# Local attention with a spectral gate on one core: sine tables moved ahead of batch 0, other PSUM banks for its transposes, pairs 2 and 3 loaded by another queue

## Chip, cores and metric

The kernel runs on one core of one Trainium2 chip, in one launch. The metric is the device time in microseconds (us), taken as the median of several runs; the profile is one further execution with the hardware profiler on.

## The reference

Two operators are joined. The first is attention over q, k, v of shape (4 batches, 8 heads, 768 positions, 64 dims). A position sees the 8 global keys and the last 96 keys (its own among them), and a distance times a slope of the head is taken off the scores:

```
scores = q @ k^T / sqrt(64) - slope[h] * dist        (only kept keys)
a = softmax(scores);  x = (a @ v), heads side by side  -> (4, 768, 512)
```

The second is a gate with a circular convolution along the 768 positions, done with a Fourier transform of each of the 512 columns:

```
x1, x2, x3 = split(x @ w_proj)                        # w_proj 512 x 1536
conv = irfft(rfft(x2) * rfft(filter_fft))
out = (x1 * conv * x3) @ w_out
```

All inputs and the output are float32 in HBM. On the chip the work is done in float16 with float32 sums.

## The kernel before

**Stages.** The work goes by batch. For a batch, `attention` (line 378) makes the 512 x 768 tile `xT`, and `hyena` (line 544) makes the output from it. The emitter writes attention of batch 0 alone, then four times hyena of batch b together with attention of batch b+1. `weave` (line 304) takes such streams, cut into steps by their `yield`s, and writes their steps in turn, each stream in even paces over its share of the stage. With hyena of batch 0 a third stream runs, `filter_stage` (line 328): it makes the sine tables `fwd` of the Fourier transform, the spectrum of the filter and the inverse tables. No planner stands behind this: each engine carries out its instructions in just the order that the program writes them, and waits at the first that is not ready.

**Attention.** Four pairs of heads follow each other. For a pair, PE transposes q and k (`transpose_q`, `transpose_k`) into PSUM, ACT copies out `QT` and DVE copies out `KT`. `weights` makes the scores of seven key blocks in three groups `sc(i, 0..2)`, ACT takes the exponential into `E` (line 499), and DVE multiplies it with the mask one step later (lines 508 and 511). `values` multiplies with v (lines 519 and 524), DVE divides by the row sum (lines 528 and 529), `transpose_x` turns the result, and ACT copies it to `xT`. All transposes use one PSUM bank, tag "tr" with one buffer; three banks with the tag "mm" serve projections and the Fourier transform, one double bank "s" the scores, two "av" the values.

**Batch 0.** It starts cold. `load_first` issues eight loads of 384 KB from SP (q and k of four pairs, float32), and `cast_first` has DVE bring each to float16 (line 143). Six staging buffers hold them. The masks are made on the way from a table of distances that POOL and DVE build (`distances`, `masks`). v of batch 0 comes from POOL's DMA queue, which casts to float16 as it goes: eight DMAs (lines 105 and 108). When they have all landed, DVE copies the global rows into six further places (line 425), and only then can `values` start. Behind v, POOL issues the three loads of `w_proj` (line 163), then k and q of batch 1, the filter `fl`, v of batch 1, and so on. On POOL's queue a DMA waits for the landing of the eighth one before it. Matmuls on a tile of zeros (`busy`, line 270) fill PE's gaps in batch 0.

**Sine tables.** In four parts a = 0..3, PE makes the products frequency times position as integers in PSUM (`dft_angles`, lines 241 to 248), ACT rounds them over S with a large constant (line 252), DVE takes the remainder in two instructions (lines 257 and 260, put some steps later by `after`), and ACT takes the sine (line 268). Exp and Sin need different tables in ACT, so each change of the function is an ACT_TABLE_LOAD.

Of the kernel before, what the change touches and what calls it, by code (L numbers as in the profile page):

```python
# [17 lines left out]
P = 128  # L18
NG = 8
# [25 lines left out]
class Fused:  # L45
# [79 lines left out]
    def load_first(self):  # L125


        nc, D = self.nc, self.D
        self.first = []
        for hp in range(4):  # L130
            hs = slice(2 * hp, 2 * hp + 2)
            for eng, src in ((nc.sync, self.q), (nc.sync, self.k)):
                st = self.stage([P, 2, 6, D])
# [13 lines left out]

    def stage(self, shape):
        t = self.mp.tile([P, 768], F32, tag="stg", bufs=6)
# [25 lines left out]
    def distances(self):  # L175
# [3 lines left out]
        dg = self.mp.tile([P, n], F32, tag="p1", name="dg")  # L179
        for ap, w, first in ((dg, n, NG), (dm[:, 2, n - 48:n], 48, NG + o)):  # L180
            g.iota(ap, pattern=[[1, w]], base=first, channel_multiplier=-1,
                   allow_small_or_imprecise_dtypes=True)

            for sgn, off in ((1, 0), (-1, NL - 1)):
                if w == 48 and sgn < 0:
                    continue
                g.affine_select(ap, ap, pattern=[[sgn, w]], base=off + sgn * first,
                                channel_multiplier=-sgn, compare_op=Alu.is_ge, fill=HUGE)

        g.affine_select(dm[:, 2, n - 48:n], dm[:, 2, n - 48:n], pattern=[[0, 48]],  # L190
                        base=-NG - o, channel_multiplier=1, compare_op=Alu.is_ge, fill=HUGE)
# [3 lines left out]
        v.memset(dm[0:NG, :, 0:KL], float(NL))  # L195
        v.memset(dm[0:NG, :, KL:n], HUGE)
        v.memset(dm[0:NG, 2, n - 48:n], float(NL))
        d0 = dm[0:NG, 0, 0:KL]
        v.memset(d0, HUGE)
        for sgn, off in ((1, 0), (-1, NL - 1)):  # L200
            g.affine_select(d0, d0, pattern=[[sgn, KL]], base=off, channel_multiplier=-sgn,
                            compare_op=Alu.is_ge, fill=float(NL))
        self.dm = dm
# [21 lines left out]
    def dft_angles(self, a):  # L225
# [29 lines left out]
    def dft_fold(self, k, th, an):  # L255
        if k == 0:
            self.nc.vector.tensor_scalar(th, th, MAGIC, -float(self.S), op0=Alu.subtract,
                                         op1=Alu.mult)
        else:
            self.nc.vector.tensor_add(th, th, an)  # L260

# [8 lines left out]
    def busy(self, n):  # L270


        if n:
            pt = self.mm()
            for _ in range(n):
                self.nc.tensor.matmul(pt, self.idle[:, 0:P], self.idle, start=True, stop=True)  # L276
# [51 lines left out]
    def filter_stage(self):  # L328
        self.fwd = self.cp.tile([P, 3, 6, P], F16)
        ths = []  # L330
        for a in range(4):
            ths.append(self.dft_angles(a))
            for k in range(2):
                self.after(k + 1, lambda k=k, a=a: self.dft_fold(k, *ths[a]))
            yield 1
        yield 1
        yield 1
        for a in range(4):
# [39 lines left out]
    def attention(self, qt, kt, vt, xT, xa, xb, first=None):  # L378
# [13 lines left out]
        def sc(i, g):  # L392
            if i < n:
                self.weights(i, g, qk[i][0], qk[i][1])
                if first and g > 0 and i + 1 < n:
                    self.masks(2 * i + 1 + g)
# [8 lines left out]
        def trx(i):  # L405
            self.transpose_x(i, xn.pop(i), xT)
            if i == n - 1:
# [4 lines left out]
        def cast(i):  # L412
            if first and i < n:
                cst[i] = self.cast_first(i)

        if first:
            cst[0] = first
        trq(0)
        yield 1
        cast(1)  # L420
        trk(0)
        yield 1
        for i in range(n + 1):
# [3 lines left out]
            for live, fn in ((i < n, lambda: sc(i, 0)),  # L427
                             (i + 2 < n and first, lambda: cast(i + 2)),
                             (i + 1 < n, lambda: trk(i + 1)),
# [5 lines left out]
                             (i == n, lambda: None),  # L435
                             (i > 0, lambda: trx(i - 1))):
                if live:
# [5 lines left out]
    def butterfly(self, j, xT, xa, xb):  # L443
        h, hs = self.S // 2, slice(j, j + 2)
        self.nc.vector.tensor_add(xa[:, hs, :], xT[:, hs, 0:h], xT[:, hs, h:])
        self.nc.vector.tensor_sub(xb[:, hs, :], xT[:, hs, 0:h], xT[:, hs, h:])

    def transpose_q(self, hp, qt, first):
# [3 lines left out]
        tq = self.ps.tile([P, 1024], F16, tag="tr", bufs=1)  # L452
        src = qt if first else qt[:, :, hs, :]
# [9 lines left out]
    def transpose_k(self, hp, kt, first):  # L463
        nc, S = self.nc, self.S
        hs = slice(2 * hp, 2 * hp + 2)
        KT = self.ap_.tile([P, 7 * P], F16, tag="kT")
        tk = self.ps.tile([P, 1024], F16, tag="tr", bufs=1)
        if first:
# [61 lines left out]

    def transpose_x(self, hp, xn, xT):
        nc = self.nc
        tx = self.ps.tile([P, 1024], F16, tag="tr", bufs=1)
        for t in range(7):
# [136 lines left out]
    def emit(self):  # L671
        nc, cp = self.nc, self.cp
        self.load_first()
        qkv = self.batch_tiles()
        self.ident = cp.tile([P, P], F16)
        make_identity(nc, self.ident)
        self.idle = self.sp.tile([P, 512], F16, bufs=1)
        nc.vector.memset(self.idle, 0.0)  # L678
        self.E = []
        for i in range(2):  # L680
# [4 lines left out]
            self.E.append(et)  # L685
        warm = self.sp.tile([1, 2], F32, bufs=1)
        nc.vector.memset(warm, 0.0)
        nc.scalar.activation(warm, warm, Act.Exp)
        self.busy(6)
        self.distances()  # L690
        cast = self.cast_first(0)
        self.masks(0)
        self.masks(1)
        self.dft_rows()
        self.load_tiles(qkv[2], self.v, 0)
        self.load_weights()
        x = self.new_x()
        self.weave((self.attention(*qkv, *x, first=cast), 34, 0, 1))
# [52 lines left out]
```

## Time and profile before

| | |
|---|---|
| device time, median of 3 runs | 240.21 us (237.61 to 240.92) |
| the profiled execution: its own time, its span | 236.61 us, 234.8 us |
| mean granted TensorE clock | 0.962 of 2.4 GHz |
| busy: PE, DVE, ACT, POOL | 197.1, 151.2, 152.8, 72.7 us |
| instructions | 4267 |

The span runs from the first to the last instruction; the 1.8 us between it and the execution's own time lie outside of them. Busy time counts an engine's instructions, not its waits. A busy share is a mean over stages with different limits, so the stages are looked at one by one below. "Idle before" in a row is the time for which that engine stood still ahead of that instruction, with what released it.

### The profile page before, as it was taken

The numbers are of one execution on the slowest core, as the hardware profiler recorded it, in microseconds if no ns is written. First come the engines' busy times: TensorE is split into PE (matmuls) and PEld (weight loads), VectorE is DVE, ScalarE is ACT, GpSimd is POOL, SyncE is SP. The second block draws the span as 40 slices with busy tenths as digits, with TensorE's granted clock in tenths as the row PEclk, the third lists the DMA queues.
The fourth block names the chain that finished last, engine by engine and source line by source line (L and its number), as shares of the span: only waits on it lengthen the run. The fifth ranks groups of instructions, "written<-read, shape, count | busy, mean of one in ns | idle before, by whom it ended". The sixth has DMA issues, their size and how long they took to land.

```text
span 234.8 us, 4267 instructions
## 1 busy us (share of the span) xinstructions
PE 197.1 (84%) x1665; PEld 105.8 (45%) x1665; DVE 151.2 (64%) x324; ACT 152.8 (65%) x246; POOL 72.7 (31%) x98
## 2 busy tenths in 40 slices
PE   6383887785598688976999999999999999998983
PEld 2141554342245444552446556644456565454541
DVE  6744677585258749986137999933599996049550
ACT  3473486477856547664687868577887885664743
POOL 6969399498940000009955100000000000000000
PEclk9999599999689979999999999999999999999999
DMA  6999999999996000009999900052000002400016
GB/s 192 348 132 189 180 152 184 137 164 154 142 117 29 6 0 0 3 0 69 221 221 123 96 9 3 1 194 77 0 3 0 3 1 93 178 0 0 3 43 228
DMA packets 79573, 21.69 MB, mean 92 GB/s; under 512 B 71328, under 2 KB 76480, under 8 KB 79552
## 3 DMA queue, kind: packets, MB, share of 16 engines
q0 software_dynamic: 73584, 11.67, 94.3%
q1 hardware_dynamic: 5968, 9.74, 12.4%
q8 instruction: 13, 0.21, 0.4%
q14 instruction: 8, 0.07, 0.1%
HBM read 26.48 MB, written 6.29 MB: 140 GB/s over the span
## 4 chain that ended last, share of the span: by engine, by line
DVE 33%; PE 31%; DMA 12%; ACT 11%; issue 5%; POOL 5%; POOLq 0%; DVEq 0%; ACTq 0%
DMA vt<-in_v_dram 7%; PE pt L650 7%; PE pt L554 6%; PE pt L568 5%; DVE xn L529 5%; DMA w<-in_moe_w_proj_dram 5%; DVE g L559 5%; PE pt L324 4%; ACT E_105 L499 2%; POOL qt L119 2%; PE tk L480 2%; ACT QT L460 2%; PE pt L632 2%; DVE y L640 2%; DVE E_108 L511 2%
## 5 line engine op out<-in xcount | busy, mean ns | idle before, releaser
L554 PE MATMUL pt<-xT,w 128*128 128x384 f16 x256 | 47.9, 333 | 0.0
L554 PEld LDWEIGHTS <-w 128*128 128x128 f16 x256 | 23.7, 99 | 16.5 <-issue 2.9
L105 POOL DMA_DIRECT2D vt<-in_v_dram x28 | 25.3, 909 | 9.3 <-DMA qt<-in_q_dram 5.5
L499 ACT ACTIVATE E_105<-sp 128x864 f16<-128x864 f32 x24 | 21.5, 898 | 8.9 <-PE sp L492 8.2
L492 PE MATMUL sp<-QT,KT 64*128 64x216 f16 (+2 forms) x224 | 18.4, 257 | 8.7 <-ACT E_105 L499 4.4
L499 ACT ACTIVATE E_108<-sp 128x864 f16<-128x864 f32 x24 | 21.5, 894 | 5.1 <-PE sp L492 4.6
L650 PE MATMUL pt<-wo,y 128*128 128x512 f16 x96 | 22.2, 379 | 2.6 <-DVE y L643 1.7
L653 ACT ACTIVATE t<-pt 128x512 f32<-128x512 f32 x24 | 14.3, 597 | 12.8 <-PE pt L650 12.6
L105 POOL DMA_DIRECT2D kt<-in_k_dram x21 | 19.4, 945 | 5.1 <-DMA w<-in_moe_w_proj_dram 4.3
L529 DVE TENSOR_TENSOR xn<-o,rc 128x448 f16<-128x448 f32 x32 | 20.0, 624 | 1.1
L324 PE MATMUL pt<-dst,fwd 128*128 128x512 f16 x72 | 19.9, 396 | 0.0
L632 PE MATMUL pt<-inv,X 128*128 128x384 f16 x96 | 18.5, 326 | 1.1 <-DVE X L593 1.1
L492 PEld LDWEIGHTS <-KT 64*128 64x128 f16 x224 | 7.7, 96 | 25.2 <-issue 19.9
L537 ACT COPY xT<-tx 128x768 f16<-128x768 f16 x16 | 12.8, 797 | 9.8 <-PE tx L536 9.8
L596 ACT CAST X<-pt 128x512 f16<-128x512 f32 x24 | 14.1, 588 | 6.8 <-PE pt L324 6.3
L570 ACT CAST dst<-pt 128x512 f16<-128x512 f32 x24 | 14.2, 594 | 6.5 <-PE pt L568 6.5
L276 PE MATMUL pt<-idle 128*128 128x512 f16 x39 | 17.2, 482 | 1.2 <-DVE idle L678 1.2
L511 DVE TENSOR_TENSOR E_105<-E_105,mask 128x864 f16<-128x864 f16 x16 | 9.7, 603 | 11.9 <-ACT E_105 L499 11.7
L119 POOL DMA_DIRECT2D qt<-in_q_dram x18 | 15.8, 922 | 0.7 <-DMA kt<-in_k_dram 0.7
L650 PEld LDWEIGHTS <-y 128*128 128x128 f16 x96 | 8.8, 98 | 13.4 <-DVE y L643 3.1
L481 DVE COPY KT<-tk 128x896 f16<-128x896 f16 x12 | 7.4, 615 | 11.2 <-PE tk L480 11.2
L536 PE MATMUL tx<-ident,xn 128*128 128x128 f16 x112 | 9.4, 226 | 5.7 <-DVE xn L529 4.8
(228 smaller groups left out, 378.5 us busy)
## 6 DMA issues: line engine op xcount, KB each, us to landing
out_dram<-t SPq DMA_DIRECT2D x24, 256.0 KB, 2.4
vt<-in_v_dram POOLq DMA_DIRECT2D x24, 128.0 KB, 8.0
kt<-in_k_dram POOLq DMA_DIRECT2D x18, 128.0 KB, 7.3
qt<-in_q_dram POOLq DMA_DIRECT2D x18, 128.0 KB, 7.3
t<-in_q_dram SPq DMA_DIRECT2D x4, 384.0 KB, 6.9
t<-in_k_dram SPq DMA_DIRECT2D x4, 384.0 KB, 7.8
w<-in_moe_w_proj_dram POOLq DMA_DIRECT2D x3, 512.0 KB, 9.0
fl<-in_moe_filter_fft_dram POOLq DMA_DIRECT2D x1, 768.0 KB, 9.7
```

Of the source, the lines that this page charges most:

```text
L105: g.dma_start(dst[P - (hi - lo):P, t, :, 0:D], src[b, :, lo:hi, :].rearrange("h p d -> p h d"))
L119: g.dma_start(qt[:, t], self.q[b, :, P * t:P * t + P, :].rearrange("h p d -> p h d"))
L276: self.nc.tensor.matmul(pt, self.idle[:, 0:P], self.idle, start=True, stop=True)
L324: self.nc.tensor.matmul(pt, self.fwd[:, kt, s, :], src[:, kt, :], start=(kt == 0), stop=(kt == 2))
L492: nc.tensor.matmul(sp[:, hh, off:off + w], KT[64 * hh:64 * hh + 64, o:o + P], QT[64 * hh:64 * hh + 64, KL * m:KL * m + w], start=(off == 0 ...
L499: nc.scalar.activation(eo, sp[:, :, 0:432].rearrange("p h (m w) -> p h m w", m=2), Act.Exp, scale=self.scale)
L511: nc.vector.tensor_mul(eo, eo, mk[:, :, 0:2] if gi == 0 else mk[:, :, 1:3])
L529: nc.vector.tensor_mul(xn[:, :, hh, :], o[:, :, 0:D], rc.to_broadcast([P, 7, D]))
L554: nc.tensor.matmul(pt[:, 0:h], self.w[:, c, o + P * j:o + P * j + P], xT[:, c, h * s:h * s + h], start=(c == 0), stop=(c == 3))
L632: nc.tensor.matmul(pt[:, 0:h], X[:, s, cs], self.inv[:, s, :], start=(s == slots[0]), stop=(s == slots[-1]))
L650: nc.tensor.matmul(pt, y[:, c, P * t:P * t + P], self.wo[:, c, :], start=(c == 0), stop=(c == 3))
L653: nc.scalar.mul(ot, pt, osc)
```

## The change

1. The sine tables are made at the start of the program, while the first q and k are on their way: `dft_rows`, the four `dft_angles` and the folds stand in `emit`, two sine activations ahead of the first `trq`, two right behind it. The warm-up activation is Sin instead of Exp. ACT takes the large constant off again in a second activation, and DVE's two instructions per part become one. The filter stream keeps its last ten steps and gets the share 0.12 to 0.4 of its stage.
2. In batch 0, `tr()` gives the transposes of q, k and x a buffer of "mm" (three banks), and `busy` writes to "tr" instead.
3. Only pairs 0 and 1 are loaded by SP as float32. Pairs 2 and 3 are loaded from POOL's queue, behind v and ahead of `w_proj`, and arrive as float16; DVE still brings them into another layout.
4. Smaller moves: `masks(0)` and `masks(1)` come behind the first exponential; the casts of a later pair stand at the end of a pair's steps instead of behind its first scores; two of the distance table's steps use a tile of their own, so POOL no longer waits for DVE in their middle; two of the six first `busy` matmuls stay.

```diff
+    def load_pairs(self, h0, eng, dt):
+        for hp in (h0, h0 + 1):
...
+            for src in (self.q, self.k):
+                st = self.stage([P, 2, 6, D], dt)
...
         nc.scalar.activation(th, an, Act.Copy, bias=MAGIC, scale=1.0 / S)
+        nc.scalar.activation(th, th, Act.Copy, bias=-MAGIC)
...
+    def dft_fold(self, th, an):
+        self.nc.vector.scalar_tensor_tensor(th, th, -float(self.S), an, op0=Alu.mult,
+                                            op1=Alu.add)
...
     def filter_stage(self):
-        for a in range(4):
-            ths.append(self.dft_angles(a))
...
-            self.dft_sines(a, ths[a][0])
         yield from self.filter_spectrum()
         yield from self.inverse_tables()
...
+    def tr(self, first):
+        if first:
+            return self.ps.tile([P, 1024], F16, tag="mm", bufs=3, name="tr")
+        return self.ps.tile([P, 1024], F16, tag="tr", bufs=1, name="tr")
...
-        nc.scalar.activation(warm, warm, Act.Exp)
-        self.busy(6)
+        nc.scalar.activation(warm, warm, Act.Sin)
+        self.busy(2)
+        self.dft_rows()
...
+        ths = [self.dft_angles(a) for a in range(4)]
+        for a in range(4):
+            if a == 2:
+                cast = self.cast_first(0)
+            self.dft_fold(*ths[a])
+        for a in range(2):
+            self.dft_sines(a, ths[a][0])
         self.load_tiles(qkv[2], self.v, 0)
+        self.load_pairs(2, nc.gpsimd, F16)
         self.load_weights()
...
-                streams.insert(0, (self.filter_stage(), 16, 0.0, 0.42))
+                streams.insert(0, (self.filter_stage(), 10, 0.12, 0.4))
```

On ACT, from the program's start to the first exponentials (L numbers are lines of each kernel's own file; `th` is an angle table, `fwd` the sine table, `sp` scores), there stood:

```order
L688 ACT_TABLE_LOAD
L688 ACTIVATE warm<-warm 1x2
L208 ACTIVATE mask<-dm 128x648 x2
L457 COPY QT<-tq 128x768
L499 ACTIVATE E_105<-sp 128x2x2x216 x2
```

and there stands now:

```order
L258 ACTIVATE th<-an 128x768
L259 ACTIVATE th<-th 128x768
L272 ACTIVATE fwd<-th 128x512 x2
L462 COPY QT<-tr 128x768
L272 ACTIVATE fwd<-th 128x512
L272 ACTIVATE fwd<-th 128x3x256
L504 ACT_TABLE_LOAD
L504 ACTIVATE E_104<-sp 128x2x2x216
L214 ACTIVATE mask<-dm 128x648 x2
```

The last two of eight roundings are shown; all four sines and one table load are now ahead of the first exponential, and the two masks behind it.

On DVE, around the copy of v's global rows (`vt<-vt`, line 425 before, 424 now; `t<-t` is the cast or copy of a pair's q and k, `KT<-tk` and `KT<-tr` the copies of k's transposes), there stood:

```order
L508 TENSOR_TENSOR E_105<-E_105,mask 128x2x216 x2
L425 COPY vt<-vt 8x3120
L511 TENSOR_TENSOR E_105<-E_105,mask 128x2x2x216
L143 CAST t<-t 128x768 x2
L511 TENSOR_TENSOR E_108<-E_108,mask 128x2x2x216
L474 COPY KT<-tk 128x6x120
```

and there stands now:

```order
L513 TENSOR_TENSOR E_104<-E_104,mask 128x2x216 x2
L146 COPY t<-t 128x768 x2
L516 TENSOR_TENSOR E_104<-E_104,mask 128x2x2x216
L424 COPY vt<-vt 8x3120
L479 COPY KT<-tr 128x6x120
```

The two copies of pair 2 (before: the casts of pair 3 stood behind v) now stand ahead of v's copy.

On POOL's queue, behind the eight DMAs of v of batch 0, there stood:

```order
L105 DMA vt<-in_v_dram 128x8x64 x6
L163 DMA w<-in_moe_w_proj_dram 128x4x512 x3
L96 MEMSET vt 128x56
```

and there stands now:

```order
L105 DMA vt<-in_v_dram 128x8x64 x6
L137 DMA t<-in_q_dram 128x2x384
L137 DMA t<-in_k_dram 128x2x384
L137 DMA t<-in_q_dram 128x2x384
L137 DMA t<-in_k_dram 128x2x384
L166 DMA w<-in_moe_w_proj_dram 128x4x512 x3
L96 MEMSET vt 128x56
```

Four DMAs are put between v and `w_proj`; all later loads keep their order behind them.

## Rows read from the trace of the kernel before

**Rows 1.** Engines by stage: length, then busy time (count) of PE, PEld, DVE, ACT, POOL, clock, DMA, GB/s.

```profile
44.20:114.60 70.40, 55.50 (x452) 28.77 (x452) 46.64 (x91) 45.91 (x74) 29.83 (x37) 0.93 1.37 71
114.60:157.60 43.00, 41.83 (x397) 23.33 (x395) 31.30 (x67) 32.58 (x54) 10.14 (x12) 1.00 1.29 97
```

**Rows 2.** The same view, three stretches of the stage from 44.2 us on.

```profile
44.20:56.30 12.10, 10.56 (x81) 4.95 (x81) 8.70 (x16) 8.38 (x13) 10.76 (x14) 1.00 2.82 155
56.30:62.30 6.00, 1.61 (x7) 0.41 (x7) 1.32 (x3) 5.94 (x9) 5.22 (x7) 0.80 2.86 149
62.30:69.50 7.20, 6.91 (x33) 3.22 (x32) 4.23 (x8) 4.18 (x8) 4.74 (x6) 0.69 3.56 121
```

**Rows 3.** Timeline of ACT: start, us, engine, line, operation, tiles.

```profile
56.33 1.28 ACT L268 ACT_TABLE_LOAD   x1
57.62 2.40 ACT L268 ACTIVATE fwd<-th 128x512 f16<-128x512 f32 x4
60.04 1.28 ACT L499 ACT_TABLE_LOAD   x1
61.33 0.89 ACT L499 ACTIVATE E_105<-sp 128x864 f16<-128x864 f32 x1
```

**Rows 4.** Groups of instructions between 44.2 and 62.3 us: busy, mean ns | idle before.

```profile
L260 DVE TENSOR_TENSOR th<-th,pt 128x512 f32<-128x512 f32 x3 | 2.1, 687 | 0.2
L257 DVE TENSOR_SCALAR th<-th 128x512 f32<-128x512 f32 (+1 forms) x4 | 1.9, 481 | 1.3 <-ACT th L252 1.3
L252 ACT ACTIVATE th<-pt 128x512 f32<-128x512 f32 x3 | 1.8, 599 | 0.0
```

**Rows 5.** Timeline of PE: an angle part, a wait, two gates, the inverse tables.

```profile
44.63 0.40 PE L241 MATMUL pt<-row 1*128 1x512 f16 x1
...
45.23 1.04 PE L568 MATMUL pt<-w,xa 128*128 128x512 f16 x4
...
53.79 0.36 PE L492 MATMUL sp<-QT,KT 64*128 64x216 f16 x4 [1.33 <-DVE th L260]
...
62.75 2.74 PE L554 MATMUL pt<-xT,w 128*128 128x384 f16 x8
...
67.05 1.46 PE L554 MATMUL pt<-xT,w 128*128 128x384 f16 x8
...
80.94 0.49 PE L286 MATMUL tp<-ident,fwd 128*128 128x128 f16 x6 [1.45 <-DVE inv L288]
```

**Rows 6.** Timeline of batch 0 on ACT and DVE.

```profile
11.05 0.89 ACT L499 ACTIVATE E_105<-sp 128x864 f16<-128x864 f32 x1 [3.42 <-PE sp L492]
...
20.58 1.02 DVE L425 COPY vt<-vt 8x3120 f16<-8x3120 f16 x1 [5.42 <-DMA vt<-in_v_dram]
22.04 1.01 DVE L143 CAST t<-t 128x768 f16<-128x768 f32 x2
...
24.58 0.18 DVE L528 RECIPROCAL rc<-o 128x7 f32<-128x7 f32 x1
...
25.54 0.80 ACT L457 COPY QT<-tq 128x768 f16<-128x768 f16 x1 [5.60 <-PE tq L455]
```

**Rows 7.** Line 105, 5.8 to 6.9 us: v's first DMA, issue to landing.

```profile
DMA to landing us min/median/max: 9.0/9.0/9.0
```

**Rows 8.** Line 105, 105.8 to 106.7 us: a like DMA of batch 3.

```profile
DMA to landing us min/median/max: 3.4/3.4/3.4
```

**Rows 9.** DMA queues 5.9 to 10.3 us: packets, MB, packet time over 16 engines.

```profile
q1 hardware_dynamic: 1122, 1.62, 104.0%
```

**Rows 10.** DMA queues 12.5 to 15 us.

```profile
q0 software_dynamic: 2437, 0.31, 403.5%
```

**Rows 11.** DMA queues 20.5 to 24.5 us.

```profile
q0 software_dynamic: 834, 0.82, 123.9%
```

**Rows 12.** Timeline of POOL: the six loads of q of batch 1.

```profile
29.05 5.25 POOL L119 DMA_DIRECT2D qt<-in_q_dram  x6
```

**Rows 13.** DMA issues 30 to 34 us: KB each, us to landing.

```profile
qt<-in_q_dram POOLq DMA_DIRECT2D x5, 128.0 KB, 6.6
```

More of the change, by code (lines that the diff above doesn't have):

```diff
@@ L125, in load_first @@
     def load_first(self):
-        nc, D = self.nc, self.D
         self.first = []
-        for hp in range(4):
+        self.load_pairs(0, self.nc.sync, F32)
+    def load_pairs(self, h0, eng, dt):
+        D = self.D
+        for hp in (h0, h0 + 1):
             hs = slice(2 * hp, 2 * hp + 2)
-            for eng, src in ((nc.sync, self.q), (nc.sync, self.k)):
-                st = self.stage([P, 2, 6, D])
+            for src in (self.q, self.k):
+                st = self.stage([P, 2, 6, D], dt)
                 eng.dma_start(st.rearrange("p h r d -> p h (r d)"),
@@ L146, in cast_first, with stage @@
         return out
-    def stage(self, shape):
-        t = self.mp.tile([P, 768], F32, tag="stg", bufs=6)
+    def stage(self, shape, dt=F32):
+        t = self.mp.tile([P, 768], dt, tag="stg", bufs=6)
         n = 1
@@ L179, in distances @@
         dg = self.mp.tile([P, n], F32, tag="p1", name="dg")
[L180 to L188, printed above, removed]
@@ L190, in distances @@
-        g.affine_select(dm[:, 2, n - 48:n], dm[:, 2, n - 48:n], pattern=[[0, 48]],
-                        base=-NG - o, channel_multiplier=1, compare_op=Alu.is_ge, fill=HUGE)
+        d0 = self.mp.tile([NG, KL], F32, tag="p1", name="d0")
+        v.memset(d0, HUGE)
+        d6 = dm[:, 2, n - 48:n]
+        g.iota(dg, pattern=[[1, n]], base=NG, channel_multiplier=-1,
+               allow_small_or_imprecise_dtypes=True)
+        for sgn, off in ((1, 0), (-1, NL - 1)):
+            g.affine_select(dg, dg, pattern=[[sgn, n]], base=off + sgn * NG,
+                            channel_multiplier=-sgn, compare_op=Alu.is_ge, fill=HUGE)
+            g.affine_select(d0, d0, pattern=[[sgn, KL]], base=off, channel_multiplier=-sgn,
+                            compare_op=Alu.is_ge, fill=float(NL))
@@ L196, in distances @@
         v.memset(dm[0:NG, :, KL:n], HUGE)
[L197 to L202, printed above, removed]
+        v.memset(d6[0:NG], float(NL))
+        v.tensor_copy(dm[0:NG, 0, 0:KL], d0)
         self.dm = dm
@@ L273, in busy @@
         if n:
-            pt = self.mm()
+            pt = self.ps.tile([P, 512], F32, tag="tr", bufs=1)
             for _ in range(n):
@@ L394, in sc @@
                 self.weights(i, g, qk[i][0], qk[i][1])
+                if first and i + g == 0:
+                    self.masks(0)
+                    self.masks(1)
                 if first and g > 0 and i + 1 < n:
@@ L405, in trx @@
         def trx(i):
-            self.transpose_x(i, xn.pop(i), xT)
+            self.transpose_x(i, xn.pop(i), xT, first)
             if i == n - 1:
@@ L416, in attention @@
         if first:
-            cst[0] = first
+            cst[0], ths = first
         trq(0)
+        if first:
+            for a in (2, 3):
+                self.dft_sines(a, ths[a][0])
         yield 1
+        trk(0)
         cast(1)
-        trk(0)
         yield 1
@@ L427, in attention @@
             for live, fn in ((i < n, lambda: sc(i, 0)),
-                             (i + 2 < n and first, lambda: cast(i + 2)),
                              (i + 1 < n, lambda: trk(i + 1)),
@@ L435, in attention @@
                              (i == n, lambda: None),
-                             (i > 0, lambda: trx(i - 1))):
+                             (i > 0, lambda: trx(i - 1)),
+                             (i + 2 < n and first, lambda: cast(i + 2))):
                 if live:
@@ L451, in transpose_q @@
         QT = self.ap_.tile([P, S], F16, tag="qT")
-        tq = self.ps.tile([P, 1024], F16, tag="tr", bufs=1)
+        tq = self.tr(first)
         src = qt if first else qt[:, :, hs, :]
@@ L466, in transpose_k @@
         KT = self.ap_.tile([P, 7 * P], F16, tag="kT")
-        tk = self.ps.tile([P, 1024], F16, tag="tr", bufs=1)
+        tk = self.tr(first)
         if first:
@@ L529, in values, with transpose_x @@
         nc.vector.tensor_mul(xn[:, :, hh, :], o[:, :, 0:D], rc.to_broadcast([P, 7, D]))
-    def transpose_x(self, hp, xn, xT):
+    def transpose_x(self, hp, xn, xT, first):
         nc = self.nc
-        tx = self.ps.tile([P, 1024], F16, tag="tr", bufs=1)
+        tx = self.tr(first)
         for t in range(7):
@@ L685, in emit @@
             self.E.append(et)
-        warm = self.sp.tile([1, 2], F32, bufs=1)
-        nc.vector.memset(warm, 0.0)
-        nc.scalar.activation(warm, warm, Act.Exp)
-        self.busy(6)
+        self.ident = cp.tile([P, P], F16)
+        make_identity(nc, self.ident)
         self.distances()
[L691 to L694, printed above, removed]
+        qkv = self.batch_tiles()
+        self.fwd = cp.tile([P, 3, 6, P], F16)
+        ths = [self.dft_angles(a) for a in range(4)]
[4 more added lines that the diff above has]
+        for a in range(2):
+            self.dft_sines(a, ths[a][0])
         self.load_tiles(qkv[2], self.v, 0)
+        self.load_pairs(2, nc.gpsimd, F16)
         self.load_weights()
         x = self.new_x()
-        self.weave((self.attention(*qkv, *x, first=cast), 34, 0, 1))
+        self.weave((self.attention(*qkv, *x, first=(cast, ths)), 34, 0, 1))
         loads = [qkv, self.load_batch(1)]
```

28 lines of the change are left out of this document (10 added, 18 removed).

## The prediction

> **What bounds the kernel now.** I read the busy times by stage first, then the stage that is out of line in finer pieces, then the timelines of the engines that wait there. Hyena of batch 1 with attention of batch 2 takes 43.0 us, and PE is busy for 41.83 of them: that is a stage at PE's bound, and nothing in the change touches it. The same pair of streams one batch earlier, with the filter stream beside it, takes 70.4 us with PE busy for 55.5 [rows 1]. So some 15 us of that stage are waits, and part of PE's busy time there ran at a lower clock. The reader is to look for what PE waits for between 44 and 70 us.
>
> In finer pieces, PE is busy 10.56 of 12.1 us, then only 1.61 of 6.0, then 6.91 of 7.2 at a mean granted clock of 0.69 [rows 2]. ACT's timeline names the hole: a table load of 1.28 us, four sines of 2.40, the load back of 1.28, and only at 61.33 us the exponential for which the scores wait [rows 3]. Before the hole, DVE works on the angles, and PE's scores at 53.79 us stood 1.33 us behind such an instruction [rows 5].
>
> Batch 0, the first 44.2 us, is bound by waits in another way: DVE stands 5.42 us until v has landed, copies it from 20.58 us on, and the first division by a row sum comes at 24.58; ACT idles 5.60 us meanwhile [rows 6].
>
> **The change part by part, the filter stage.** The sums are made in the profiled execution's time, 236.61 us.
>
> A, 44.2 to 56.3 us. The angles leave PE, ACT and DVE. On PE a part stands from 44.63 to 45.23 us, where the next projection begins [rows 5], so 0.6 us, and four parts are 2.4; the wait of 1.33 for DVE goes as well. Together 3.7. PE's remaining 8.2 us are near what ACT and DVE keep: ACT 8.38 less 1.8 for three roundings and an estimated 0.8 for the larger fourth, DVE 8.70 less 2.1 and 1.9 and an estimated 1.0 for the larger addition [rows 2, 4], so 5.8 and 3.7. I take 3.5, with 1.5 and 4.0 as ends, since ACT's copies may be late for PE in so dense a stretch.
>
> B, 56.3 to 62.3 us. From 56.33 to 61.33 ACT does nothing but tables and sines: 5.0 us [rows 3]. What was hidden in the hole (two sums of the filter's halves on DVE, three matmuls on PE, 1.61 us of PE in all [rows 2]) must now find its place. I take 4.2; ends 2.5 and 5.0.
>
> C, 62.3 to 69.5 us. After the hole the clock was at 1.2 GHz for part of this stretch: the same eight matmuls of a gate took 2.74 us at 62.75 and 1.46 at 67.05 [rows 5]. That gate gives back 1.28 and the three filter matmuls behind it about half as much, 1.9 in all if PE stays busy. I take 1.7; ends 0 and 2.
>
> D, the inverse tables. Their three transposes share the bank "tr" with attention's; PE stood 1.45 us for one of them [rows 5]. With the shorter filter stream they stand further apart. I take 1.2, with a loss of 1 and a gain of 3 as ends.
>
> The filter's copies now fall into a denser stretch: a cost of 0.5, ends 0 and 1.5. The stage gains 3.5 + 4.2 + 1.7 + 1.2 - 0.5 = 10.1.
>
> On the table loads the rows show 1.28 us each, and the first sine begins 0.01 us behind its load [rows 3]. The Trainium skill (ScalarE: Activation LUTs, What ACT_TABLE_LOAD costs) counts about 2.66 us for a switch, of which about half is a drain behind the load. The trace has no such drain; by the page the two switches here would have cost 2.7 us more than they did, so term B goes by the rows.
>
> **The change part by part, batch 0.** Ahead of the first exponential ACT now has eight roundings (0.6 us each by the group, an estimated 0.8 for the two larger, so 5.2), four sines (2.40) and a load (1.28) [rows 3, 4]. With the first product ready near 2.7 us (an estimate) and the first copy of q among the sines, the exponential comes at about 11.9 instead of 11.05 us. What hides the 0.9 us is ACT's idle time of 5.60 ahead of 25.54 [rows 6]. Without that cover it costs 0.9, and up to 4 if folds on DVE and sines on ACT wait for each other.
>
> DVE gets four folds of about 0.7 us [rows 4] ahead of the first copy of k. The four angle parts on PE stand in a start where PE waits anyway.
>
> v's landing. v's first DMA took 9.0 us from issue to landing, a like one into an idle queue 3.4 [rows 7, 8]. From v's issue to 10.3 us no packet of POOL's queue ran: only SP's did, at 1.62 MB in 4.4 us [rows 9]. The four loads that leave SP are 1.57 MB, so v's packets may start about 3 us earlier, no more, since v's issue at about 5.2 us then sets the start. Behind them stand four DMAs, 192 KB each in float16. `w_proj`, the nearest row, landed 0.82 MB in 4 us [rows 11]: 0.94 us each. So v is there at about 17.5 us and pair 2 at 19.5.
>
> DVE waits for pair 2 first, in front of a mask (0.6) and v's copy: 19.5 + 0.3 + 0.6 = 20.4, hardly before today's 20.58. Only then does the move pay: the two casts of 1.01 us behind v are gone [rows 6], so the first division comes near 23.0 instead of 24.58. The three banks for transposes add perhaps 0.5. I take E = 2.0. The ends are far apart: a loss of 3.5 (pair 2 lands as late as 25, as it would with v's 9.0 us between issue and landing, behind an issue near 13 and two more landings), a gain of 4 (DVE does not wait at all, and only the exponentials bind).
>
> On the queues the rows show that v's packets did not run until SP's traffic was nearly through [rows 9, 10]. The Trainium skill (DMA: Bandwidth & Descriptors, Issuing engines are not separate DMA queues) says that DMAs of all issuing engines run on the same 16 DMA engines and interleave, so that another issuer saves only its issue time. The bytes ahead of pair 2's landing stay the same, and by that rule E would be near zero: the sum would be 226.5 instead of 224.5.
>
> POOL's queue grows by four transfers, 3.8 us, and loses the 3 us by which v starts earlier. q of batch 1 has its last issue near 33.4 us and lands 6.6 later, at 40.0 [rows 12, 13]; that becomes 41. Attention of batch 1 begins at about 42.2 instead of 44.2, so a margin of one microsecond hides it. Without it, E loses its further gains.
>
> **The sum.** 10.1 + 2.0 = 12.1 us; 236.61 - 12.1 = 224.5 us in the profiled execution. The median of the runs is 240.21, 3.6 more than that execution. The same 3.6 added gives 228.1 us, my prediction. A measurement of this kernel can tell about 2% from no change.
>
> **The rivals.**
>
> R1, pair 2 holds DVE. The copies of pair 2 wait in DVE's order ahead of the mask and v's copy. v's own rows speak for it: 9.0 us between issue and landing [rows 7], then one tile a microsecond: 2437 packets in 2.5 us, 1024 to a tile [rows 10]. Against it speak the lighter SP queue and the 3.4 us of an idle one [rows 8]. E is then -3.5 and the time 228.1 + 5.5 = 233.6.
>
> R2, the hole was not what bound the filter stage. DVE has 46.64 us of work there and ACT 45.91 in 70.4 [rows 1], and the filter's copies go from ACT to DVE; if they keep PE waiting wherever they stand, A and B give 1.5 and 2.5, C and D nothing, and E nothing as in the queue rule: 240.2 - 4.0 + 0.5 = 236.7, within 2%. Against it: once the hole is over, the gates run one behind the other [rows 2].
>
> R3, slower. The place is DVE's wait for k of pair 2; its price is one microsecond for each that it lands after 19.5, since PE, ACT and all of batch 0 stand behind v's copy. It decides from 19.5 + 12.1 = 31.6 us on; at 35 us the time is 228.1 + 15.5 = 243.6. For it: each of the four waits for a landing of v before it can be issued, and casts as it goes. Against it: it would need over 18 us from its issue, twice v's 9.0.
>
> R4, better. DVE does not wait, PE keeps its clock, and the ends of D and E come true: 228.1 - 3.8 = 224.3.
>
> **How the numbers follow.** Forecast 0.62, R1 0.17, R2 0.10, R3 0.04, R4 0.07. The range reaches from a little under R4 to a little over R1, 222 to 235; R2 and R3 are left out, with the outer tails of the others. Faster by over 2% means below 235.4: the forecast and R4 wholly and 0.13 of R1, so 0.82. Within 2%: R2 and the rest of R1, 0.14. Slower: 0.04.
>
> **What would show it.** Right would be: no ACT_TABLE_LOAD after 15 us; no stretch of several microseconds after batch 0 with PE under half busy; a clock near 1.00 from there to 70 us; the stage that took 70.4 us near 60; v's copy on DVE near 20 us, with a wait for pair 2's DMA in front of it, and the first division near 23. E is wrong if v's copy comes after 22 us or if PE's first transpose of batch 1 waits for q. The filter terms are wrong if the scores of batch 1 wait for DVE or ACT at work on the filter's copies, or for `fl` itself. The whole is wrong if batch 0 ends later than at 46 us, or if the stage behind it shortens by less than 5.

## The result, and the profile after

The kernel takes 223.03 us after the change (median of 4 runs, 221.65 to 224.31) against 240.56 before it (237.61 to 242.75) on the same chip: a ratio of 0.931, with a 95% interval from 0.919 to 0.943. The profiled execution took 222.22 us against 236.61, so 14.4 us less. Some executions below are a few us longer than others of the same kernel, at a lower clock: the medians include them, the ratios leave them out, and since the profiled executions of e1 and e3 were such ones, of these two only the times are used.

The page of the profile after, its granted TensorE clock in 40 slices:

```profile
span 220.4 us, 4260 instructions
...
PEclk9999999999999999999999999999999999999998
```

Before, the clock was at 0.74 and 0.58 from 20 to 25 and from 25 to 30 us, at 0.50 and 0.82 from 60 to 70, and at 0.88 and 0.78 from 80 to 90. Now it holds its upper level, 2.4 GHz, to the last slice (mean 0.997).

Engines by stage, with the columns of [rows 1]. The first row is the stage with the filter stream, the second the stage behind it; then come three pieces of the first, which answer to [rows 2]:

```profile
41.16:99.70 58.54, 48.53 (x434) 26.34 (x434) 41.67 (x83) 38.58 (x65) 31.18 (x39) 1.00 1.75 97
99.70:142.70 43.00, 41.83 (x397) 23.33 (x395) 31.30 (x67) 32.57 (x54) 10.12 (x12) 1.00 1.14 98
41.16:51.10 9.94, 9.45 (x70) 4.48 (x70) 5.81 (x10) 7.36 (x13) 6.05 (x9) 1.00 3.07 151
51.10:58.00 6.90, 5.21 (x35) 2.70 (x36) 4.36 (x8) 5.10 (x10) 5.61 (x7) 1.00 2.02 165
58.00:67.00 9.00, 7.78 (x78) 4.71 (x76) 7.18 (x16) 5.30 (x9) 8.08 (x11) 1.00 2.74 139
```

Read it against [rows 1, 2]. Batch 0 ends 3.0 us earlier (41.16 for 44.20). The filter stage is 11.9 us shorter (58.54 for 70.40). The stage behind it, 43.00 us with PE busy for 41.83, is the same to the hundredth. Of the 11.9 us, PE's own busy time gives 7.0 (48.53 for 55.50) and its waits 4.9 (10.0 for 14.9). The stretch with PE busy for 1.61 of 6.0 us is gone; the emptiest of the three pieces now has 5.21 of 6.90.

Timeline of ACT after, the start, where the tables now are:

```profile
8.30 1.13 ACT L272 ACTIVATE fwd<-th 128x512 f16<-128x512 f32 x2
9.34 0.78 ACT L462 COPY QT<-tr 128x768 f16<-128x768 f16 x1
10.02 1.36 ACT L272 ACTIVATE fwd<-th 128x512 f16<-128x512 f32 x2
11.40 1.28 ACT L504 ACT_TABLE_LOAD   x1
12.70 0.89 ACT L504 ACTIVATE E_104<-sp 128x864 f16<-128x864 f32 x1
```

The first exponential moves from 11.05 [rows 6] to 12.70 us. That costs nothing visible, since what binds batch 0 comes later, on DVE. The timeline of DVE after, the same place as in [rows 6]:

```profile
17.85 0.57 DVE L146 COPY t<-t 128x768 f16<-128x768 f16 x1 [1.51 <-DMA t<-in_q_dram]
18.81 0.36 DVE L146 COPY t<-t 128x768 f16<-128x768 f16 x1 [0.40 <-DMA t<-in_k_dram]
19.09 0.60 DVE L516 TENSOR_TENSOR E_104<-E_104,mask 128x864 f16<-128x864 f16 x1
19.61 0.95 DVE L424 COPY vt<-vt 8x3120 f16<-8x3120 f16 x1
...
22.25 0.20 DVE L533 RECIPROCAL rc<-o 128x7 f32<-128x7 f32 x1
```

DVE now waits for pair 2 (1.51 and 0.40 us) where it stood 5.42 us for v. The casts of 1.01 us behind v's copy are gone, and the first division comes at 22.25 instead of 24.58.

Three rows of PE's timeline show what is late next while the filter stream runs: scores, sums of values, and the last of the inverse tables' three groups of transposes:

```profile
52.01 0.36 PE L497 MATMUL sp<-QT,KT 64*128 64x216 f16 x4 [1.11 <-ACT E_104 L504]
...
59.90 0.20 PE L524 MATMUL o<-vt,E_104 128*128 128x65 f16 x1 [0.86 <-DMA vt<-vt]
...
69.56 0.50 PE L290 MATMUL tp<-ident,fwd 128*128 128x128 f16 x6 [1.01 <-ACT xT L542]
```

None of these waits is over 1.2 us. The longest of the stage comes later, 1.68 us at 78.98 for DVE's division (`xn`); before, the same one took 1.05 us at 93.89.

### The profile page after: what moved, and what is told of

Same layout as the page of the kernel before. It is cut to its first block, busy times and chain, and to the rows that moved or that the text cites. A ratio compares the mean times of both kernels' runs of the same rounds, so it can differ in the third digit from the quotient of the medians.

```text
span 220.4 us, 4260 instructions
## 1 busy us (share of the span) xinstructions
PE 193.8 (88%) x1661; PEld 104.5 (47%) x1661; DVE 148.5 (67%) x321; ACT 153.3 (70%) x249; POOL 75.8 (34%) x102
## 4 chain that ended last, share of the span: by engine, by line
PE 31%; DVE 30%; DMA 18%; POOL 8%; ACT 7%; issue 4%; POOLq 0%; DVEq 0%; SPq 0%
PE pt L655 7%; PE pt L559 7%; DMA w<-in_moe_w_proj_dram 5%; DMA vt<-in_v_dram 5%; PE pt L573 5%; DVE g L564 5%; DVE xn L534 4%; DMA fl<-in_moe_filter_fft_dram 4%; DMA vt<-vt 3%; PE pt L637 3%; POOL qt L119 2%; ACT E_104 L504 2%; PE sp L497 2%; DVE E_107 L516 2%; PE pt L328 2%
## 5 line engine op out<-in xcount | busy, mean ns | idle before, releaser
L559 PE MATMUL pt<-xT,w 128*128 128x384 f16 x256 | 46.8, 326 | 0.6 <-DVE g L564 0.4
L105 POOL DMA_DIRECT2D kt<-in_k_dram x21 | 19.6, 953 | 5.8 <-DMA w<-in_moe_w_proj_dram 4.8
L328 PE MATMUL pt<-dst,fwd 128*128 128x512 f16 x72 | 18.9, 380 | 0.0
L542 ACT COPY xT<-tr 128x768 f16<-128x768 f16 x16 | 12.8, 798 | 7.7 <-PE tr L541 7.6
L280 PE MATMUL pt<-idle 128*128 128x512 f16 x35 | 16.4, 475 | 1.4 <-DVE warm L682 1.2
L486 DVE COPY KT<-tr 128x896 f16<-128x896 f16 x12 | 7.4, 619 | 10.9 <-PE tr L485 10.9
L541 PE MATMUL tr<-ident,xn 128*128 128x128 f16 x112 | 9.0, 220 | 5.2 <-DVE xn L534 4.8
## 6 DMA issues: line engine op xcount, KB each, us to landing
w<-in_moe_w_proj_dram POOLq DMA_DIRECT2D x3, 512.0 KB, 10.3
```

The lines of the kernel that those rows point to most:

```text
L105: g.dma_start(dst[P - (hi - lo):P, t, :, 0:D], src[b, :, lo:hi, :].rearrange("h p d -> p h d"))
L328: self.nc.tensor.matmul(pt, self.fwd[:, kt, s, :], src[:, kt, :], start=(kt == 0), stop=(kt == 2))
L559: nc.tensor.matmul(pt[:, 0:h], self.w[:, c, o + P * j:o + P * j + P], xT[:, c, h * s:h * s + h], start=(c == 0), stop=(c == 3))
```

## The experiments

The theory is that of the prediction: the gain comes from the tables' work in the filter stage, in terms A to D (angles, hole, clock, bank of the inverse tables), and to a small part, term E, from batch 0. Its rival gives the loads and banks of batch 0 a gain of their own; others put the stage's loss on something that the tables merely stood beside.

"Stage" is from here on the time from PE's first transpose of batch 1's q to the end of ACT's last output copy of batch 0: 70.98 us before, 59.13 after. "Batch 0" is where that first transpose stands: 44.20 and 41.16. A hundredth of the ratio is 2.4 us. A ratio compares with runs of the kernel before on the same chip; e5 to e8 ran on another chip than e1 to e4 and e9 to e12, so rows of the two groups are compared by their ratios rather than by their medians.

| kernel | batch 0 ends | stage | clock | median us | ratio to before, 95% |
|---|---|---|---|---|---|
| before | 44.20 | 70.98 | 0.962 | 240.56 | |
| after | 41.16 | 59.13 | 0.997 | 223.03 | 0.931 (0.919 to 0.943) |
| e1 before again | | | | 239.23 | 0.999 (0.994 to 1.003) |
| e2 tables only | 41.76 | 58.79 | 0.999 | 223.85 | 0.933 (0.925 to 0.942) |
| e3 all but the tables | | | | 238.19 | 0.985 (0.973 to 0.996) |
| e4 all but the loads | 42.09 | 59.01 | 1.000 | 223.08 | 0.929 (0.918 to 0.941) |
| e5 hole back | 40.55 | 66.30 | 0.983 | 228.55 | 0.960 (0.956 to 0.965) |
| e6 before, inverse tables' bank | 45.44 | 68.73 | 0.971 | 235.64 | 0.990 (0.986 to 0.994) |
| e7 e2, casts in old places | 43.54 | 58.81 | 1.000 | 224.40 | 0.942 (0.937 to 0.946) |
| e8 before, PE kept busy | 45.05 | 71.28 | 0.970 | 237.84 | 0.999 (0.995 to 1.003) |
| e9 after again | 41.95 | 60.70 | 0.992 | 223.28 | 0.932 (0.927 to 0.937) |
| e10 v's rows on DVE | 41.03 | 59.02 | 0.988 | 224.18 | 0.935 (0.930 to 0.941) |
| e11 e10, inverse tables' bank | 41.32 | 61.17 | 0.974 | 223.22 | 0.931 (0.926 to 0.937) |
| e12 e4 with e10 | 40.36 | 60.72 | 0.992 | 224.49 | 0.936 (0.930 to 0.942) |

### The three parts of the change (e2, e3, e4)

e2 keeps the tables and undoes the banks and the loads; e4 undoes the loads alone (the lines on `load_pairs`).

```diff
         self.load_pairs(0, self.nc.sync, F32)
+        self.load_pairs(2, self.nc.sync, F32)
...
-            pt = self.ps.tile([P, 512], F32, tag="tr", bufs=1)
+            pt = self.mm()
...
-        if first:
-            return self.ps.tile([P, 1024], F16, tag="mm", bufs=3, name="tr")
...
-        self.load_pairs(2, nc.gpsimd, F16)
```

> The changed kernel with parts 2 and 3 undone: tables made at the start, but eight float32 loads from SP and one transpose bank in batch 0. Theory 1 (the filter stage is most of it): the stage behind batch 0 takes 58 to 60 us instead of 70.4, batch 0 ends at 43.5 to 45.5 us, and the profiled time is 224.5 to 226. Rival (early tables also bring batch 0's gain, by keeping PE and its clock up): batch 0 ends at 41 to 42 us and the time is that of the changed kernel, 222 to 223. Rival (the front work is not hidden without the lighter SP queue): batch 0 ends after 47 us, time over 228.

> The changed kernel with part 3 undone: all eight float32 loads from SP, tables early, three banks. If the loads are what brings v earlier: v's copy on DVE comes at 20 to 21 us instead of 19.6, batch 0 ends at 43 to 44 us, profiled time 224 to 225.5. By the rule that all issuers share the same DMA engines the loads' place matters little: v's copy within 0.5 us of 19.6, time 222 to 223.

e3 keeps banks and loads and puts the tables back into the filter stream (with the first masks and the fillers at the start as before).

```diff
     def filter_stage(self):
+        for a in range(4):
+            ths.append(self.dft_angles(a))
...
+        for a in range(4):
+            self.dft_sines(a, ths[a][0])
         yield from self.filter_spectrum()
...
-                streams.insert(0, (self.filter_stage(), 10, 0.12, 0.4))
+                streams.insert(0, (self.filter_stage(), 16, 0.0, 0.42))
```

> The changed kernel with part 1 undone: parts 2 and 3 alone, the tables in the filter stage as before. Theory 1: batch 0 ends near 41 to 42 us, the stage behind it takes 69 to 71 us again, profiled time 233 to 235. Rival (the filter stage's length came from the wait for loads that parts 2 and 3 move): the stage takes under 66 us and the time is under 230.

Tables alone give 0.933, the whole change 0.931 and 0.932 (e9): the other two parts add nothing that can be measured. Without the tables 1.5% is left, on two of e3's four runs, with an interval from 0.4 to 2.7%. What e2 and the whole change share besides the tables are the smaller moves of part 4; e7 takes up one of them, the order in DVE's stream, and the others were not undone alone.

### The hole and its clock (e5, e8)

e5 gives the kernel after its hole back: four sines without use at the start of the filter stream, and so two table loads. They write a tile that nothing reads.

```diff
     def filter_stage(self):
+        sc = self.sp.tile([P, 768], F16, bufs=1)
+        for n in (512, 512, 512, 768):
+            self.nc.scalar.activation(sc[:, 0:n],
...
+                                      Act.Sin, scale=1.0e-3)
```

> The changed kernel with ACT's hole put back: at the start of the filter stream ACT takes four more sines of the old sizes from the masks into a tile that nothing reads, with the two table loads that this takes (5 us on ACT by the rows of before); the angles stay at the program's start. Theory 1 (the hole is term B, and the clock falls behind it): the stage behind batch 0 grows by 4 to 7 us, the time to 226 to 229, and the granted clock falls to about 0.96 to 0.98. Rival (the tables' gain is the angles' work on PE and DVE, the hole would be hidden): the stage grows by less than 2 us, the clock stays at 0.99.

The stage grew by 7.2 us against after, and the ratio by 2.9 hundredths, about 7 us. (Against e9 the stage grew by 5.6, but there its last matmuls ran at the lower clock for 1.7 us longer; the section on e6 shows such a case.) Of the 7.2, 0.6 are two waits of PE for q of batch 1 (0.21 and 0.41), since here batch 0 ended at 40.55, before q was there. So 6.6 are left for the hole and its clock. The window of e5 from 51 us on:

```profile
51.00:58.00 7.00, 0.88 (x5) 0.35 (x6) 0.78 (x2) 6.15 (x10) 6.03 (x8) 0.80 1.98 165
```

and the same window of the kernel after:

```profile
51.00:58.00 7.00, 5.21 (x35) 2.70 (x36) 4.36 (x8) 5.20 (x10) 5.71 (x7) 1.00 2.01 165
```

PE's timeline of e5 behind the hole:

```profile
53.88 0.81 PE L328 MATMUL pt<-f,fwd 128*128 128x512 f16 x3 [3.27 <-ACT dst L580]
...
57.93 0.54 PE L502 MATMUL sp<-QT,KT 64*128 64x216 f16 x4 [3.23 <-ACT E L509]
58.40 2.74 PE L564 MATMUL pt<-xT,w 128*128 128x384 f16 x8
```

PE waits 3.27 and 3.23 us for ACT, and the next gate takes 2.74 us, as in [rows 5], where it takes 1.46 at the upper clock. ACT spends 5.4 us on the hole here: two loads of 1.28 and four sines of 2.83 in all, with copies between the sines and the load back. The hole costs about its own length and then the slow stretch behind it.

e8 tries the clock by itself: twelve matmuls without use after the sines of the kernel before, and twelve behind the first filter product. The hole stays.

```diff
             self.dft_sines(a, ths[a][0])
+        self.busy(12)
         yield from self.filter_spectrum()
...
             self.forward(s, f2[0], f2[1], evac)
+            if s == 0:
+                self.busy(12)
```

> The kernel before with 24 matmuls on zeros added in PE's queue around ACT's hole (12 ahead of the filter's first product, 12 behind it; 0.2 us each at full clock, so 2.5 us twice, about what PE waits there: 1.6 and 2.5 us). Nothing is removed. Theory (term C is the clock that falls in the hole): the granted clock of the stretch 62 to 70 us is near 1.00 instead of 0.69, the mean clock over 0.97, and the time falls by 1 to 2 us although PE has more to do. Rival (the clock costs nothing there, the copies out of PSUM bind): no gain, or a loss of up to 2 us.

PE's timeline of e8:

```profile
57.41 2.96 PE L276 MATMUL pt<-idle 128*128 128x512 f16 x12
...
62.12 2.75 PE L276 MATMUL pt<-idle 128*128 128x512 f16 x12
64.80 0.36 PE L495 MATMUL sp<-QT,KT 64*128 64x216 f16 x4
...
70.74 0.36 PE L495 MATMUL sp<-QT,KT 64*128 64x216 f16 x4
```

From 60 to 70 us the clock was 1.00, where before has 0.50 and 0.82. But the second filler ended later than the scores were ready: they stood 19.75 us after the stage's start instead of 18.07. From these scores to the next it then took 5.94 us (64.80 to 70.74), where before it took 7.27 (62.27 to 69.54, rows below) with the same work in between. So the upper clock gave back 1.3 us of the 1.7, and the stage is as long as it was. This prices the clock term at 1.3 us; that a filler can earn it is not shown, since this one was put too late.

### The inverse tables' bank (e6)

The kernel before, with the inverse tables' transposes in the three banks "mm" instead of the one bank "tr":

```diff
         for sp in range(3):
-            tp = self.ps.tile([P, 1024], F16, tag="tr", bufs=1)
+            tp = self.ps.tile([P, 1024], F16, tag="mm", bufs=3)
```

> The kernel before with one thing changed: the inverse tables' transposes use the three banks of mm instead of the one bank tr that attention's transposes use. If term D (2.8 us in the after profile against 1.2 forecast) is this bank: PE's wait of 1.45 us for the copy of the inverse tables goes, the stage behind batch 0 shortens by 2 to 3 us, time 234 in a profile like that of before. Rival (term D is the clock, which before falls again at 80 to 90 us, or the steps' other places): less than 1 us.

The stage became 2.25 us shorter, and the whole 1.0% faster (0.6 to 1.4). PE's timeline of the kernel before, right behind the last of [rows 5], with its wait of 1.45 us:

```profile
82.08 0.55 PE L536 MATMUL tx<-ident,xn 128*128 128x128 f16 x7 [0.65 <-DVE inv L288]
83.52 0.56 PE L286 MATMUL tp<-ident,fwd 128*128 128x128 f16 x6 [0.89 <-ACT xT L537]
...
84.49 1.46 PE L324 MATMUL pt<-dst,fwd 128*128 128x512 f16 x3
```

and of e6, the same instructions:

```profile
81.29 0.55 PE L536 MATMUL tx<-ident,xn 128*128 128x128 f16 x7
81.69 0.50 PE L286 MATMUL tp<-ident,fwd 128*128 128x128 f16 x6
...
82.41 0.82 PE L324 MATMUL pt<-dst,fwd 128*128 128x512 f16 x3
```

In the kernel before, three waits stand in a row (1.45, 0.65, 0.89), and then the clock is low: three matmuls of batch 0's own Fourier transform (`dst`) take 1.46 us instead of 0.82. In e6 these waits and the slow matmuls are gone together; its clock from 80 to 90 us is 1.00.

The 2.25 us understate the place. The last output products of batch 0, before and in e6:

```profile
109.85 4.71 PE L650 MATMUL pt<-wo,y 128*128 128x512 f16 x21 [1.02 <-DVE y L643]
107.14 6.39 PE L650 MATMUL pt<-wo,y 128*128 128x512 f16 x21 [1.01 <-DVE y L643]
```

From the stage's start they stand at 65.65 and 61.70 us, so e6 is 3.95 us ahead here; then its 21 matmuls take 1.68 us longer, at a clock of 0.50 from 108 to 110 us, behind the same wait. The same happens in e9, e11 and e12 (6.30 to 6.39 us) and not in after, e2, e4, e5, e7, e8 and e10 (4.71), so of two executions of the changed kernel, after and e9, only one has it. What decides it stays open. Stages of the table can be compared to better than 1.7 us only where these matmuls ran at the same clock.

### The places of the casts (e7)

e2, but the casts of pairs 1 to 3 stand where the kernel before has them:

```diff
-        trk(0)
         cast(1)
+        trk(0)
...
             for live, fn in ((i < n, lambda: sc(i, 0)),
+                             (i + 2 < n and first, lambda: cast(i + 2)),
...
-                             (i > 0, lambda: trx(i - 1)),
-                             (i + 2 < n and first, lambda: cast(i + 2))):
+                             (i > 0, lambda: trx(i - 1))):
```

> The tables-only kernel with the casts of a later pair back at their old places (behind a pair's first scores, ahead of v's copy or behind it as before). The tables-only kernel ended batch 0 at 41.8 us against 44.2 before. If the casts' places bring that: batch 0 ends at 43 to 44 us, and the first division is 1 us later. Rival (the front work on PE and ACT keeps the clock at 1.00 from 20 to 30 us, where before it fell to 0.58, and that alone brings it): batch 0 ends within 0.5 us of 41.8.

DVE's timeline of e7:

```profile
21.20 0.96 DVE L425 COPY vt<-vt 8x3120 f16<-8x3120 f16 x1 [3.90 <-DMA vt<-in_v_dram]
...
22.61 1.01 DVE L147 CAST t<-t 128x768 f16<-128x768 f32 x2
...
25.16 0.18 DVE L532 RECIPROCAL rc<-o 128x7 f32<-128x7 f32 x1
```

and of e2:

```profile
21.00 0.96 DVE L425 COPY vt<-vt 8x3120 f16<-8x3120 f16 x1 [2.04 <-DMA vt<-in_v_dram]
...
23.50 0.19 DVE L532 RECIPROCAL rc<-o 128x7 f32<-128x7 f32 x1
```

In e2 two casts and a mask fit into DVE's wait for v (2.04 us are left of 3.90) and no longer stand between v's copy and the division: these are 2.50 us apart instead of 3.96. Batch 0 ends 1.8 us earlier, 41.76 for 43.54, with the loads still on the old queue; 1.5 of it are the casts and the mask. The ratios, 0.933 and 0.942, differ by as much (2.1 us), but their intervals overlap.

### How steady the kernels are (e1, e9)

Both are unchanged files. e1 was to show whether the medians of before lie above its profiled execution because its clock is lower in most runs.

> The kernel before, unchanged, run again for the clock of each of its runs. Its profiled execution took 236.6 us, its other runs 237.6 to 242.8. Theory: PE's pauses (the hole of the sines, the wait for v) let the clock fall for a stretch that differs from run to run, so the longer runs are those of the lower mean clock: 0.962 for a span of 234.8 us, and about 0.94 for a span of 239. Rival: the runs differ by something else (transfers), and spans and clocks do not go together.

> The changed kernel, unchanged, beside the next three on the same chip: about 222 us in a profile, 223 in the median, clock 0.99 or more in every run.

The 10 runs of e1 lie at 237.5 to 245.9 us, those of after and e9 at 221.7 to 224.5. Over the 32 runs of before that the ratios use, time and clock go together only weakly (a correlation of -0.36). The six at a clock of 0.962 to 0.964 took 237.33 to 239.02 us, where the profiled execution took 236.61 at 0.962. So the clock does not account for that gap, and its cause stays open. e9's DVE waits 2.69 and 0.57 us for pair 2, and v's copy stands at 20.80 instead of 19.61: the same program, 1.2 us apart.

### What is late next (e10, e11, e12)

PE waits 0.86 us at 59.90 for `vt<-vt`, SP's copy of v's global rows. In e10 DVE makes these rows for batch 1, as it does for batch 0. e12 does the same without the loads (e4); e11 adds the edit of e6 to e10.

```diff
-        if b > 0:
+        if b > 1 or b == 1 and src is not self.v:
...
-            if first and i == 1:
+            if (first or rows) and i == 1:
```

> The changed kernel; the global rows of v of batch 1 are copied by DVE ahead of the first use (1 us on DVE) instead of by a DMA of SP, which takes 7.3 us behind v's landing and for which PE waited 0.9 us. Theory (the loads put behind v push v of batch 1 back by 0.8 us, and that wait eats what they gain in batch 0): the wait goes, batch 0 stays at 41.2 us, the time falls by 0.5 to 0.9 us. Rival (a copy of 1 us in DVE's order there delays the filter's copies by as much): no change.

> The same, and the inverse tables' transposes on the mm banks, as in the run that changed only these in the kernel before (2.2 us there). In the after profile PE waits 1.0 us for that bank. Expected: another 0.5 to 1.0 us less than with v's rows alone, near 221 in a profile. Rival: the three mm banks are then late for the projections, no change.

> The changed kernel with part 3 undone (eight loads from SP) and v's rows of batch 1 on DVE. There v of batch 1 lands 0.4 us earlier and PE did not wait for it. If the loads' gain in batch 0 (0.9 us) is kept once the wait for v is gone, this kernel is 0.5 to 1 us slower than the one with v's rows on DVE and the loads moved; if all issuers sharing the DMA engines is the whole story, the two are the same within 0.3 us.

The wait on the copy went, and another took its place. PE's waits in after:

```profile
PE o L524 <- DMA vt<-vt: 0.9, 1, 0.9
...
PE pt L559 <- DVE g L564: 0.4, 1, 0.4
```

and in e10:

```profile
PE pt L559 <- DVE g L564: 1.2, 1, 1.2
```

No version is measurably faster than the kernel after or e2. The inverse tables' bank, worth 2.25 us before, brings nothing measurable here: the medians of e11 and e10 differ by 0.96 us inside their intervals. e11's profiled stage is longer, not shorter, because its clock fell twice (0.79 and 0.78 from 76 to 84 us, 0.50 from 96 to 98). Its six runs show what that is worth: the three at a clock of 0.997 or more took 222.28 to 222.56 us, the two at 0.974 and 0.975 took 224.75 and 224.85. Over the 34 runs of after, e2, e4 and e9 to e12 that the ratios use, time and clock have a correlation of -0.76: what still differs between them goes mostly with the clock.

## Why the prediction was right, and where it was off

The forecast of 228.1 us named the right parts; the time is 5.1 us lower. The sum was 12.1 us against 14.4 measured between the profiled executions (11.85 in the stage and 3.0 in batch 0, less 0.5 that the later stages take longer). The rest, 2.8 us, is the step "the same 3.6 added": the kernel after lies only 0.8 us above its profiled execution (223.03 for 222.22). That a median's distance to one execution carries over was an assumption with nothing behind it.

The terms of the stage can be read one by one where attention of batch 1 and batch 0's transform take the same steps in both kernels. PE's rows of the kernel before:

```profile
55.38 0.36 PE L492 MATMUL sp<-QT,KT 64*128 64x216 f16 x6
62.27 0.54 PE L492 MATMUL sp<-QT,KT 64*128 64x216 f16 x4 [2.54 <-ACT E_105 L499]
69.54 0.36 PE L492 MATMUL sp<-QT,KT 64*128 64x216 f16 x4
78.67 0.82 PE L324 MATMUL pt<-dst,fwd 128*128 128x512 f16 x3
87.60 0.36 PE L492 MATMUL sp<-QT,KT 64*128 64x216 f16 x4
```

The same rows of the kernel after; the second of them is shown further up, at 52.01:

```profile
48.92 0.36 PE L497 MATMUL sp<-QT,KT 64*128 64x216 f16 x6
57.90 0.36 PE L497 MATMUL sp<-QT,KT 64*128 64x216 f16 x4
67.33 0.82 PE L328 MATMUL pt<-dst,fwd 128*128 128x512 f16 x3
72.08 0.36 PE L497 MATMUL sp<-QT,KT 64*128 64x216 f16 x4
```

Counted from the stage's start (44.20 and 41.16), with what each stretch gained beside its forecast:

| up to | before | after | gained here | forecast |
|---|---|---|---|---|
| third scores of the first pair | 11.18 | 7.76 | 3.4 | A 3.5 |
| first scores of the second pair | 18.07 | 10.85 | 3.8 | B 4.2 |
| its second scores | 25.34 | 16.74 | 1.4 | C 1.7 |
| a first product of batch 0's transform | 34.47 | 26.17 | -0.3 | copies -0.5 |
| second scores of the third pair | 43.40 | 30.92 | 4.2 | D 1.2 |
| end of the stage | 70.98 | 59.13 | -0.6 | |

The cuts are not sharp, since steps of the filter stream stand at other places in the kernel after. But the size that was far off is D's.

**A, angles (3.5, with 0.5 off for the filter's copies).** 3.4 by the rows, although the kernel after has by then also made a first product of the filter (48.18). No run put the angles back alone, so that the angles are its cause is argued.

**B and C, the hole and its clock (4.2 + 1.7 = 5.9).** The rows give 3.8 and 1.4, and e5, which puts the hole back into the kernel after, gives 6.6 for both. For C alone e8 gives 1.3. The trace of e5 agrees with [rows 3] on the table load: 1.28 us, and the next activation 0.01 us behind it, without the drain that the Trainium skill (ScalarE: Activation LUTs, What ACT_TABLE_LOAD costs) counts:

```profile
55.69 1.28 ACT L509 ACT_TABLE_LOAD   x1
56.98 0.89 ACT L509 ACTIVATE E<-sp 128x864 f16<-128x864 f32 x1
```

**D, the inverse tables (1.2).** Mis-sized. The rows give 4.2, of which 0.6 goes again in the longer wait for DVE's division at 78.98. That one bank can be the cause, e6 shows: 3.95 us up to the last output products, with nothing else changed. The step took one wait of 1.45 us and left out the two behind it and the matmuls at the lower clock that followed; after has one wait of 1.01 us there and none of the slow matmuls. The upper end of 3 was too low as well.

**E, batch 0 (2.0).** It came to 3.0, in the range from -3.5 to 4, but for another reason than the text gives first. The landing terms came as forecast: v's first DMA took 4.4 us from issue to landing for 9.0 [rows 7], its last landing was 3.6 us earlier, and pair 2 was there at 18.79 us, 0.7 ahead of the estimate. But e2, e4 and e12, without the moved loads, end batch 0 at 41.76, 42.09 and 40.36, and the five kernels with the loads moved and the same batch 0 (after, e5, e9, e10, e11) at 40.55 to 41.95. On the totals (223.03 for e4's 223.08) this is what the Trainium skill's rule says (DMA: Bandwidth & Descriptors, Issuing engines are not separate DMA queues): the bytes ahead of what DVE needs last stayed the same.

Two things paid. One is the casts behind v's copy, which the prediction names: e7 gives 1.5 us for their places and the mask's, and e2 shows that the DMA's cast was not needed for it. For the other the prediction has no term. From the first division to the end of batch 0 the three kernels with the old batch 0 (before, e6, e8) take 19.6 to 19.7 us, e7 18.4 and e2 18.3, so 1.2 us came with the early tables or the smaller moves beside them. From 20 to 30 us the clock is 1.00 in e7 and e2, and 0.74 and 0.58 before; that this is the reason is argued, not shown.

The 3.0 itself hangs on one execution: e6 and e8, whose batch 0 is that of before, end it at 45.44 and 45.05, not at 44.20. The banks' 0.5 was not seen. The first exponential came at 12.70 us, not at 11.9; the sum for it has no room for the copy of q among the sines, 0.78 us, and DVE's later wait covered it.

**The margin for q of batch 1** held: q lands at 40.83 us, PE starts at 41.16. It is almost used up; in e5, where batch 0 ended at 40.55, PE waited 0.6 us for q.

**The rivals.** R1 was there in kind: DVE does wait for pair 2, for 1.51 and 0.40 us, behind a landing that did not come late. R2 is refuted by e5. R3's landing would have had to be 13 us later. R4's time is the nearest, though not for its reason, since DVE does wait.

## What to carry to other kernels

A table switch in the middle of a dense stage costs more than its own length: in e5, 5.4 us of ACT's time cost 6.6, since PE ran dry and its clock was low for the next products. Follow a wait for a bank through all waits and the slow matmuls behind it before it is priced. When parts of a change come together, undo each by itself: here two of three were worth nothing measurable, and the order of two casts beside them did more for batch 0 than the new queue. Before two profiles are compared to a microsecond, see that the same matmuls ran at the same clock in both.

## What was not expected of the hardware

SP's copy of 49 KB within SBUF took 7.25 us; in that time, 52.6 to 59.9 us, POOL's queue moved 1.10 of the 1.15 MB in all. That the busy queue is the reason is not shown. On the chain of waits of the kernel after:

```profile
52.60 7.25 DMA vt<-vt
```

The clock behind one and the same pair of waits differs between executions of one program: after PE had waited 0.88 and 1.02 us for DVE, the 21 output matmuls took 4.71 us in after; in e9, after 0.88 and 1.01, they took 6.39 at a granted clock of 0.66 and 0.50 (96 to 98 and 98 to 100 us).

Landings of one and the same program vary by about a microsecond between executions (v's copy at 19.61 and 20.80 us), so moves of loads that are worth less than that cannot be told apart by one profile each.
